# Forward weave dealt anew: row transposes of the attention sweep moved behind the row sums, and a 64-token projection tile, in a fused forward and backward kernel

## The chip, the cores and the metric

The kernel runs on one core of one Trainium2 chip. The metric is the device time of one execution in microseconds (us), the median of several runs. The engines are named as the profile names them: PE is TensorE (matmuls), PEld its weight loads, DVE is VectorE, ACT is ScalarE, POOL is GpSimd, SP is the queue that issues most DMAs. `L82` is line 82 of the kernel before.

## The reference

The reference returns the output of a gated mix of two attentions and the gradients of eleven inputs. `A` is multi-query attention with 32 heads of 18 channels over 2048 tokens; `B` is a recurrent attention with 32 heads of 128 channels over 64 segments of 32 tokens, in which eight memory rows go from one segment to the next:

```python
g = _sigmoid((x * gate_w).sum(-1, keepdims=True))
a = _A_ref(x, A_wq, A_wk, A_wv, A_wo)
b = _B_ref(x, B_mem0, B_Wq, B_Wk, B_Wv, B_Wo, B_seg_len)
return g * a + (1 - g) * b
```

The recurrence in `_B_ref`, where `mem` makes each segment wait for the one before:

```python
for s in range(n_seg):
    xs = x[:, s * seg_len:(s + 1) * seg_len, :].copy()
    h = jnp.concatenate([mem, xs], axis=1)
    q = jnp.einsum('btd,dhe->bhte', h, Wq)
    k = jnp.einsum('btd,dhe->bhte', h, Wk)
    v = jnp.einsum('btd,dhe->bhte', h, Wv)
    scores = jnp.einsum('bhqe,bhke->bhqk', q, k) * scale
    scores = jnp.where(mask[None, None], scores, -1000000000.0)
    p = _softmax(scores, axis=-1)
    o = jnp.einsum('bhqk,bhke->bhqe', p, v)
    o = jnp.einsum('bhte,hed->btd', o, Wo)
    mem = o[:, :M, :].copy()
    outs.append(o[:, M:, :])
```

The gradients come from `jax.vjp` of this function.

## The kernel before

The work stands in stages that follow each other. Inside the stages named here the order on each engine is the order in which the Python code emits it.

**Token projection** (`b_proj`, lines 229 to 259). Products of 128-token tiles with the weights of B: sixteen tiles of `dO`, then `XT0 = 5` tiles times k, v and q, fifteen items. An item has eight PSUM tiles `p_pb` of 128x512, each of four matmuls over full 128-row slices and one over a 64-row tail; four such tiles are computed, then copied by DVE and ACT in turn into `p_tok` (two buffers). SP writes `p_tok` to DRAM (`kx_dram`, `vx_dram`, `qx_dram`) at the start of the next item, the last one at line 258. The tokens from 640 on are not projected here.

**Forward weave** (`weave`, line 283). Two generators take turns: `b_chain_fwd`, the recurrence of B, with 64 segments of sixteen pieces, and `a_pass1`, the attention sweep of A, with 64 blocks of sixteen steps. Place p of a segment is piece p of the chain followed by one step of the sweep (step 16s+p+2). One sweep step n emits: scores of the next step (`a_S`, one buffer in PSUM), products `a_dP`, the exponential of the next step on ACT (`a_E`, L1881), two products on DVE (`a_W`, L1914), and twelve accumulating matmuls of step n-1 (`a_acc`). So the scores of a step wait until the exponential of the step before has read `a_S`.

The pieces of the chain that matter: place 0 forms the memory rows (`row_sums`), places 1 to 3 project k in halves `("k", 0)` in PSUM tile `c_pj` and `("k", 1)` in `c_x`, 4 to 6 project q, 6 and 7 transpose, 7 to 11 project v, 8 and 9 form the scores in `px` (a `c_x` tile), place 10 forms the softmax row sums `den` there with two matmuls against a block matrix, DVE takes the reciprocal `c_rd` (L521), POOL scales (`c_pn`, L523) and expands the probabilities to block form (`c_PBm`, then `c_PBx`, both L261); place 12 multiplies them with the values (`po`, `c_x`), PBx first. Places 13 to 15 project the output (`c_pj`). `c_x` and `c_pj` have one buffer each.

A projection unit `proj("k", j, kts)` emits four matmuls of 128x32 by 512 columns for each entry of `kts`.

The chain also carries, in the 24 rows of a segment that its 8 memory rows leave free, the projection of tokens that the first stage left out (`ride`, `put_ride`, the copies in `rows_copy`): 24 tokens a segment from token 640 on.

When a block of the sweep ends, ACT copies `a_acc` to `a_acs`, and `a_post` finishes the block during the next one, piece by piece: at step 3 of sixteen (place 1) it transposes the first half of `a_acs` (`half(0)`: two 128x128 float32 transposes into `c_x`, copied to `a_tk` by ACT); at step 10 (place 8) it loads the block's queries by two DMA transposes; at step 14 (place 12) it transposes the second half (into `c_pj`, copied by DVE); at step 15 (place 13) come the small products on POOL, which read `a_tk`, and the stores. For the last block all of that follows the sweep, on DVE, with its queries loaded into the memory of `a_W`.

**Bulk of B** (`b_bulk`, lines 691 to 964). Starts after the weave: for 128 groups of four heads in 128-token tiles it transposes q, k, dO and v, forms probabilities, outputs and gradients. At its start DVE zeroes four block tiles (`mB`, L675), SP issues the loads of the first four chunks (a chunk is four groups) in the order of lines 926 to 932, and the loop over groups starts. The step of group t transposes v of group t-2, multiplies the memory values `x_vmB` for group t-3 and the memory keys `x_kmB` for t-5.

After these stages come the backward weave, the gradients of the weights and the last products; the change doesn't touch them.

Of the kernel before, what the change touches and what calls it, by code (L numbers as in the profile page):

```python
# [16 lines left out]
P = 128  # L17
# [29 lines left out]
class Kern:  # L47
# [49 lines left out]

    XT0 = 5

# [130 lines left out]
    def b_proj(self, items, n0, n1, sp, psum, extra):  # L230
        nc = self.nc
        due = []
        for n in range(n0, n1):
            w, tt = items[n]
            for m in range(n, n + 3):
                self.proj_load(items, m, sp)
            extra(n)
            for args in due:
                nc.sync.dma_start(*args)
            xt = self.px.pop((w, tt))  # L240
            Wt = self.WoT if w == "dO" else self.W[w]
            tok = sp.tile([P, J], BF16, name="p_tok", bufs=2)
            for c2 in range(2):
                cs = (2 * c2, 2 * c2 + 1)
                pb = {(c, j): psum.tile([P, 512], F32, name="p_pb", bufs=8) for c in cs for j in range(2)}
                for c, j in pb:
                    for kt in range(4):
                        self.mm(pb[c, j][:], lhsT=xt[:, kt, :],
                                rhs=Wt[0][:, kt, (2 * c + j) * 512:(2 * c + j + 1) * 512],
                                start=(kt == 0), stop=False)  # L250
                for c, j in pb:
                    r = slice(64 * j, 64 * j + 64)
                    self.mm(pb[c, j][:], lhsT=xt[r, 4, :], rhs=Wt[1][r, c, :], start=False, stop=True, tp=(64 * j, 0))
                for c, j in pb:
                    self.evac(tok[:, (2 * c + j) * 512:(2 * c + j + 1) * 512], pb[c, j][:], use="vs"[j])
            due = [(self.xtok[w][tt * P:(tt + 1) * P, :], tok[:])]
        for args in due:
            nc.sync.dma_start(*args)
# [84 lines left out]
    def b_chain_fwd(self, keep, sp, psum):  # L343
        nc = self.nc
        NSEG = self.NSEG
        hm = self.hm
        hx = keep.tile([P, 3, 64], F32, name="c_hx")
        PBm = keep.tile([P, 8, 64], BF16, name="c_PBm")
# [6 lines left out]
        def ride(s):  # L355
            t0 = self.XT0 * P + 24 * s
            return t0, max(0, min(24, self.T - t0))
# [55 lines left out]
        for s in range(NSEG):  # L413
# [50 lines left out]
            if not last:  # L464
                put_ride(s + 1)
            proj("k", 0, (0, 1))
            yield
            proj("k", 0, (2, 3, 4))
            proj("k", 1, (0,))
            if wt is not None:  # L470
# [5 lines left out]
            yield  # L476
            proj("k", 1, (1, 2, 3, 4))
            yield
# [20 lines left out]
            proj("v", 0, (2, 3))  # L499
            px = psum.tile([P, 192], F32, name="c_x", bufs=1)  # L500
            ps, den = px[:, 0:P], px[:, P:192]
# [16 lines left out]
            self.mm(den, lhsT=self.blockones[:], rhs=Et[:, 0, :], start=True, stop=False)  # L518
            self.mm(den, lhsT=self.blockones[:], rhs=Et[:, 1, :], start=False, stop=True)
            rd = sp.tile([P, 64], F32, name="c_rd", bufs=1)  # L520
            nc.vector.reciprocal(rd[:], den)  # L521
# [147 lines left out]
    def b_bulk(self, wp, vp, kp, sp, psum):  # L669
# [3 lines left out]
        mB = {w: [wp.tile([P, 4, 4, E], BF16, name=f"x_{w}mB{i}") for i in range(2)] for w in ("k", "v")}  # L673
        for t in mB["v"] + mB["k"]:
            nc.vector.memset(t[:], 0.0)  # L675
        mT = {}
# [248 lines left out]
        later = {}  # L925
        load(0, ("q", "k", "mT", "dO"))
        load(1, deep)
        load(0, ("v", "vB", "kB"))
        load(1, ("v", "vB", "kB"))
        load(2, deep + ("mT", "v"))  # L930
        for c in range(3, BQ):
            load(c, deep)
        for t in range(NG + 6):
# [4 lines left out]
            for n, st in order:  # L938
# [5 lines left out]
                if st in after and t - n >= 0 and (t - n) % 4 == 3:  # L944
                    c = (t - n) // 4
                    for w, wait in after[st]:
                        later.setdefault(t + wait, []).append((c + (BQ if w in deep else 3 if w in ("mT", "v") else 2), (w,)))
                        if wait == 0:
                            load(*later[t].pop())
            if t % 4 == 2 and t // 4 - 2 in range(NTT // 4):  # L950
                self.dl_rows(t // 4 - 2, sp, psum)
# [912 lines left out]
    def a_pass1(self, keep, sp, psum, xps):  # L1864
# [78 lines left out]
    def a_post(self, b, acs, sp, psum, dl_all):  # L1943
# [6 lines left out]
        def queries():  # L1950
            qt = sp.tile([P, 2, 2, P], BF16, name="a_qt", tag="a_W" if end else "a_qt", bufs=2 if end else 1)
            src = self.qs_blk(b, 0)
# [4 lines left out]
        def half(hf):  # L1957
            pt = psum.tile([P, 2, P], F32, name=("c_x", "c_pj")[hf], bufs=1)
            for j in range(2):
                nc.tensor.transpose(pt[:, j, :], acs[:, (2 * hf + j) * P:(2 * hf + j + 1) * P], self.identF[:])  # L1960
            self.evac(tk[:, :, :, 32 * hf:32 * hf + 32], pt[:].rearrange("p t (g c) -> p t g c", c=32), use="sv"[hf])
# [37 lines left out]
        for w in range(2):  # L1999
            eng.tensor_copy(r4[:, :, :, w, :], rl[:, w].rearrange("p t (a i) -> p a t i", i=2))  # L2000
        q4 = qt[:].rearrange("p a t (b c) -> p (a t b) c", c=32)
        eng.tensor_tensor(out=q4, in0=q4, op=ALU.mult,
                                in1=r4[:].rearrange("p a t w i -> p (a t w i)").unsqueeze(2).to_broadcast([P, 16, 32]))
        dq_.dma_start(self.qs_blk(b, 1).rearrange("a p c -> p a c"), qt[:].rearrange("p a t x -> p a (t x)"))

# [360 lines left out]
```

## Time and profile before

| what | value |
|---|---|
| time, median of 3 runs | 5284.89 us (5282.66 to 5288.88) |
| time of the profiled execution | 5276.59 us |
| its span (first to last instruction) | 5274.6 us |

Busy time of the engines in stretches of the profiled execution, us, with the granted PE clock:

| stretch, us from the start | stage | length | PE | DVE | ACT | POOL | clock |
|---|---|---|---|---|---|---|---|
| 133.5 to 390.1 | token projection | 256.6 | 254.0 | 78.8 | 66.0 | 7.8 | 1.00 |
| 391.3 to 2029.6 | forward weave | 1638.3 | 1576.7 | 1419.8 | 1358.2 | 906.6 | 1.00 |
| 2030.9 to 2050.4 | weave to bulk | 19.5 | 4.1 | 11.1 | 1.3 | 11.7 | 0.55 |
| 2050.4 to 2600.0 | bulk of B, most of it | 549.6 | 518.5 | 412.5 | 356.6 | 399.6 | 0.99 |
| 2600.0 to 5274.6 | the rest | 2674.6 | 2539.1 | 1599.5 | 1452.1 | 1186.5 | 0.99 |

A row of the timeline has the start in us, the busy time in us, the engine, the line, the operation, output and inputs, their shapes, how many instructions were merged, and in brackets the idle time before it and what ended it. Matmul ends are modelled, so the distance between starts tells more than the busy time. All matmuls of the helper `mm` stand at L82, all bfloat16 transposes at L87; the tile names tell them apart.

### The profile page before, as it was taken

Reading aid. Unit: us, or ns where it says so; the run is one execution under the profiler, and the core shown is the slowest. Engines: PE = TensorE matmul, PEld = TensorE weight load, DVE = VectorE, ACT = ScalarE, POOL = GpSimd, SP = SyncE. Lnnn points to the kernel's source line nnn. Section 1 sums busy time; section 2 is a strip of 40 time slices with the busy share of each in tenths; the row PEclk is TensorE's granted clock in tenths of the full one; section 3 lists DMA queues with packets and bytes.
Section 4 is the critical chain, followed back from the end, with each engine's and each line's share of the span. In section 5 each row is a group of like instructions: output and inputs, shape, how many; then the busy total and the mean of one; then the engine's idle time right before and its main releaser. Section 6 shows DMA issues by size and latency. Waiting matters only on the chain.

```text
span 5274.6 us, 213519 instructions
## 1 busy us (share of the span) xinstructions
PE 4994.6 (95%) x90945; PEld 2898.4 (55%) x90945; DVE 3589.9 (68%) x7121; ACT 3295.0 (62%) x4757; POOL 2553.8 (48%) x4853
## 2 busy tenths in 40 slices
PE   7999999999999998999879999999999999999999
PEld 4335555555555555777635555555554467764444
DVE  5338888888888887777778888888888831111212
ACT  4228888888888886666668888888887732110100
POOL 2005555555555555777736666666654421222213
PEclk8999999999999999999989999999999999999999
DMA  6756556655665445888866989988977769966653
GB/s 225 236 198 133 145 140 141 148 141 138 141 145 131 118 108 181 254 246 251 262 178 177 200 200 196 200 198 198 202 166 143 149 160 233 282 222 213 198 187 106
DMA packets 1119994, 961.15 MB, mean 182 GB/s; under 512 B 689966, under 2 KB 947959, under 8 KB 1109438
## 3 DMA queue, kind: packets, MB, share of 16 engines
q1 hardware_dynamic: 1020318, 709.18, 54.8%
q0 software_dynamic: 98576, 238.16, 15.0%
q8 instruction: 712, 11.67, 1.0%
q14 instruction: 244, 2.00, 0.1%
q10 hardware_dynamic: 144, 0.15, 0.0%
HBM read 521.16 MB, written 357.96 MB: 167 GB/s over the span
## 4 chain that ended last, share of the span: by engine, by line
PE 71%; ACT 9%; issue 5%; DVE 4%; DMA 4%; POOL 3%; SPq 1%; POOLq 0%; ACTq 0%; DVEq 0%
PE w_acc L82 11%; PE r_pj L82 7%; PE b_S L82 6%; PE a_S L82 6%; ACT b_E L2054 5%; PE a_acc L82 5%; PE c_pj L82 5%; PE b_acc L82 5%; PE r_x L82 5%; PE p_pb L82 4%; PE c_x L82 4%; ACT a_E L1881 3%; PE y_pdx L82 2%; PE x_tr L87 2%; PE x_po L82 1%
## 5 line engine op out<-in xcount | busy, mean ns | idle before, releaser
L2077 DVE TENSOR_TENSOR b_dS<-b_dP,b_E 128x512 bf16<-128x512 f32 x2048 | 1315.1, 684 | 220.9 <-issue 87.1
L1914 DVE TENSOR_TENSOR a_W<-a_dP,a_E 128x512 bf16<-128x512 f32 x2048 | 1313.9, 684 | 205.6 <-issue 73.0
L2054 ACT ACTIVATE b_E<-b_S 128x1024 bf16<-128x1024 f32 x1024 | 1048.8, 1024 | 284.2 <-PE b_dP L82 197.9
L1881 ACT ACTIVATE a_E<-a_S 128x1024 bf16<-128x1024 f32 x1024 | 1049.9, 1025 | 237.4 <-PE a_dP L82 193.2
L82 PEld LDWEIGHTS <-b_QS 32*128 32x128 bf16 (+1 forms) x8192 | 271.1, 92 | 521.2 <-issue 466.6
L82 PE MATMUL r_pj<-WT,r_dT 128*32 128x288 bf16 x12288 | 495.7, 286 | 3.4 <-issue 3.4
L82 PE MATMUL b_S<-b_KV,b_QS 32*128 32x512 bf16 x2048 | 405.1, 382 | 92.8 <-ACT b_E L2054 62.0
L82 PE MATMUL w_acc<-w_d,w_h 128*128 128x512 bf16 (+1 forms) x2400 | 475.0, 379 | 0.0
L82 PE MATMUL a_S<-a_QD,l_KV 32*128 32x512 bf16 x2048 | 399.3, 381 | 41.6 <-ACT a_E L1881 19.8
L82 PE MATMUL b_acc<-b_dS,b_QS 128*32 128x512 bf16 x2048 | 422.8, 392 | 0.1
L82 PE MATMUL a_acc<-a_E,l_VK 128*32 128x256 bf16 x8192 | 412.1, 278 | 5.0
L82 PE MATMUL b_acc<-b_E,b_QS 128*32 128x512 bf16 x2048 | 405.7, 393 | 0.0
L82 PE MATMUL b_dP<-b_KV,b_QS 32*128 32x512 bf16 x2048 | 402.2, 388 | 0.0
L82 PE MATMUL a_dP<-a_QD,l_KV 32*128 32x512 bf16 x2048 | 398.3, 385 | 0.2 <-DVE a_W L1914 0.2
L82 PEld LDWEIGHTS <-r_dT 128*32 128x32 bf16 x12288 | 336.3, 97 | 92.9 <-issue 6.3
L82 PEld LDWEIGHTS <-w_h 128*128 128x128 bf16 (+1 forms) x2688 | 229.3, 100 | 258.9 <-issue 9.6
L82 PEld LDWEIGHTS <-l_KV 32*128 32x128 bf16 x4096 | 149.9, 91 | 287.4 <-issue 263.9
L82 PE MATMUL a_acc<-a_W,l_WK 128*32 128x256 bf16 x4096 | 291.4, 273 | 0.4 <-DVE a_W L1914 0.3
L79 ACT CAST w_o<-w_acc 128x512 bf16<-128x512 f32 x54 | 31.7, 586 | 384.6 <-PE w_acc L82 374.8
L82 PEld LDWEIGHTS <-l_VK 128*32 128x32 bf16 x8192 | 128.9, 94 | 236.9 <-issue 233.1
L77 DVE CAST w_o<-w_acc 128x512 bf16<-128x512 f32 x54 | 37.3, 692 | 313.5 <-PE w_acc L82 298.7
L1100 POOL TENSOR_TENSOR r_kb<-r_ks,bmask 128x512 bf16<-128x512 bf16 x176 | 188.7, 1072 | 105.2 <-DMA r_ks<-px_dram 49.5
(489 smaller groups left out, 10559.6 us busy)
## 6 DMA issues: line engine op xcount, KB each, us to landing
b_QS<-qs_dram SPq DMA_DIRECT2D x256, 256.0 KB
dOx_dram<-p_tok SPq DMA_DIRECT2D x16, 1024.0 KB
c_vx<-vx_dram SPq DMA_DIRECT2D x64, 256.0 KB
krow_dram<-c_k POOLq DMA_DIRECT2D x64, 256.0 KB, 2.9
qrow_dram<-c_q POOLq DMA_DIRECT2D x64, 256.0 KB, 4.4
vrow_dram<-c_v POOLq DMA_DIRECT2D x64, 256.0 KB, 6.3
x_q<-qx_dram SPq DMA_DIRECT2D x32, 512.0 KB
x_k<-kx_dram SPq DMA_DIRECT2D x32, 512.0 KB
```

Source lines behind the costliest of these rows:

```text
L77: nc.vector.tensor_copy(out, in_)
L79: nc.scalar.copy(out, in_)
L82: return self.nc.tensor.matmul(out, lhsT, rhs, start=start, stop=stop, tile_position=tp, skip_group_check=True)
L87: return self.nc.tensor.transpose(out, in_, self.identB[b:b + nrows, b:b + nrows], tile_position=tp)
L1100: nc.gpsimd.tensor_tensor(out=B[:], in0=a[:].unsqueeze(2).to_broadcast([P, 4, 4, SEG]), in1=self.bmask[:, :, 0].unsqueeze(1).unsqueeze(3). ...
L1881: nc.scalar.activation(E_[n][:], S.pop(n)[:], ACT.Exp, scale=SCALEA)
L1914: nc.vector.tensor_tensor(out=W_[n][:, i, :], in0=dP[i][:], in1=E_[n][:, i, :], op=ALU.mult)
L2054: nc.scalar.activation(E_[n][:], S.pop(n)[:], ACT.Exp, scale=SCALEA)
L2077: nc.vector.tensor_tensor(out=D_[n][:, i, :], in0=dP[i][:], in1=E_[n][:, i, :], op=ALU.mult)
```

## The change

It does five things.

1. The ride starts at token `X0 = 576`. The fifth projection tile then has 64 tokens: its items k, v and q write two 512-column halves to the two halves of the partitions of one PSUM tile (matmuls of 128x64 at `tile_position` (0, 64j), tails of 64x64), four `p_pb` tiles instead of eight, copied by DVE and ACT in turn, and stored by two DMAs with runs of 1 KB instead of one with runs of 8 KB. Rides go on to segment 61 instead of 58.
2. `half(0)` of the block's post-processing leaves place 1. The `c_x` tile of the chain's scores becomes 448 columns wide, and its last 256 columns take the two transposes at place 10, behind the row sums `den` and ahead of the reciprocal. Its query load stays at step 10.
3. The units of the projection of k are dealt anew: before 2, 4, 4 units at places 1, 2, 3, after it 3, 4, 3.
4. At place 10 POOL expands `c_PBx` ahead of `c_PBm`.
5. Between weave and bulk: the queries of the last block are loaded five steps before the end into a `c_wt` buffer (which the chain no longer uses then), its `a_tk` goes to a buffer of `a_E`; the bulk loads v of chunk 0 ahead of chunk 1 (`load`, called by `first(t)` at the end of the step of group t, issues the rest); the four memsets and the loads of `mB` are spread over the first four groups; and the first group's q and k transposes are copied by ACT.

```diff
-    XT0 = 5
+    XT0, X0 = 5, 576
...
+            T0 = P if w == "dO" else min(P, self.X0 - tt * P)
...
+                if T0 < 128:
+                    for c in cs:
+                        pb = psum.tile([P, 512], F32, name="p_pb", bufs=8)
+                        for kt in range(4):
+                            for j in range(2):
+                                self.mm(pb[64 * j:64 * j + 64, :], lhsT=xt[:, kt, 0:64],
+                                        rhs=Wt[0][:, kt, (2 * c + j) * 512:(2 * c + j + 1) * 512],
+                                        start=(kt == 0), stop=False, tp=(0, 64 * j))
+                        for j in range(2):
+                            r = slice(64 * j, 64 * j + 64)
+                            self.mm(pb[r, :], lhsT=xt[r, 4, 0:64], rhs=Wt[1][r, c, :], start=False, stop=True,
+                                    tp=(64 * j, 64 * j))
+                        self.evac(tok[:, c * 512:c * 512 + 512], pb[:], use="vs"[c % 2])
+                    continue
...
+            if T0 < 128:
+                due = [(self.xtok[w][tt * P:tt * P + 64, :].rearrange("t (c j e) -> t c j e", j=2, e=512)[:, :, j, :],
+                        tok[64 * j:64 * j + 64, 0:2048].rearrange("t (c e) -> t c e", e=512)) for j in range(2)]
+                continue
...
-            t0 = self.XT0 * P + 24 * s
+            t0 = self.X0 + 24 * s
...
-            proj("k", 0, (0, 1))
-            yield
-            proj("k", 0, (2, 3, 4))
-            proj("k", 1, (0,))
+            proj("k", 0, (0, 1, 2))
+            yield
+            proj("k", 0, (3, 4))
+            proj("k", 1, (0, 1))
...
-            proj("k", 1, (1, 2, 3, 4))
+            proj("k", 1, (2, 3, 4))
...
-            px = psum.tile([P, 192], F32, name="c_x", bufs=1)
+            px = psum.tile([P, 448], F32, name="c_x", bufs=1)
+            self.px_rest = px[:, 192:448].rearrange("p (t c) -> p t c", t=2)
...
             self.mm(den, lhsT=self.blockones[:], rhs=Et[:, 1, :], start=False, stop=True)
+            if s:
+                self.row_T()
             rd = sp.tile([P, 64], F32, name="c_rd", bufs=1)
             nc.vector.reciprocal(rd[:], den)
...
+            self.expand(PBx[:], pn[:, 0].rearrange("p (u q) -> p u q", q=8), 8)
             self.expand(PBm[:, :, 0:32].rearrange("p u (c q) -> p u c q", q=8), pn[:, 1].rearrange("p (u q) -> p u q", q=8), 8)
-            self.expand(PBx[:], pn[:, 0].rearrange("p (u q) -> p u q", q=8), 8)
...
-        for t in mB["v"] + mB["k"]:
-            nc.vector.memset(t[:], 0.0)
...
-            self.evac(o[:], pt[:], use="s" if w in ("dO", "v") else "v")
+            self.evac(o[:], pt[:], use="s" if w in ("dO", "v") or t == 0 else "v")
...
-        load(0, ("q", "k", "mT", "dO"))
+        load(0, ("q", "k", "mT", "dO", "v"))
         load(1, deep)
-        load(0, ("v", "vB", "kB"))
-        load(1, ("v", "vB", "kB"))
-        load(2, deep + ("mT", "v"))
-        for c in range(3, BQ):
-            load(c, deep)
+
+        def first(t):
+            if t < 4:
+                nc.vector.memset(mB["vk"[t // 2]][t % 2][:], 0.0)
+                load(t % 2, ("vk"[t // 2] + "B",))
+            if t == 0:
+                load(1, ("v",))
+            elif t == 1:
+                load(2, deep)
+            elif t == 2:
+                load(2, ("mT", "v"))
+                for c in range(3, BQ):
+                    load(c, deep)
...
-                if post is not None and kt in (3, 14):
+                if post is not None and kt == 14:
                     next(post)
+                if n == NP_ - 5:
+                    self.qt_last = self.cfs.tile([P, D], BF16, name="c_wt", bufs=2)[:, 0:512].rearrange(
+                        "p (a t x) -> p a t x", a=2, t=2)
+                    for a, src in enumerate(self.qs_blk(NB - 1, 0)):
+                        nc.sync.dma_start_transpose(self.qt_last[:, a], src)
...
         def half(hf):
-            pt = psum.tile([P, 2, P], F32, name=("c_x", "c_pj")[hf], bufs=1)
+            if hf or end:
+                pt = psum.tile([P, 2, P], F32, name=("c_x", "c_pj")[hf], bufs=1)[:]
+            else:
+                pt = self.px_rest
...
         if end:
-            qt = queries()
-        tk = sp.tile([P, 2, 4, 64], F32, name="a_tk", bufs=1)
-        half(0)
-        yield
+            qt = self.qt_last
+        tk = sp.tile([P, 2, 4, 64], F32, name="a_tk", tag="a_E" if end else "a_tk", bufs=3 if end else 1)
         if not end:
             qt = queries()
+            self.row_T = lambda: half(0)
+        else:
+            half(0)
         yield
         half(1)
```

More of the change, by code (lines that the diff above doesn't have):

```diff
@@ L240, in b_proj @@
             xt = self.px.pop((w, tt))
+            T0 = P if w == "dO" else min(P, self.X0 - tt * P)
+            assert T0 in (64, P)
             Wt = self.WoT if w == "dO" else self.W[w]
@@ L346, in b_chain_fwd @@
         hm = self.hm
+        self.cfs = sp
         hx = keep.tile([P, 3, 64], F32, name="c_hx")
@@ L949, in b_bulk @@
                             load(*later[t].pop())
+            first(t)
             if t % 4 == 2 and t // 4 - 2 in range(NTT // 4):
@@ L1950, in queries @@
         def queries():
-            qt = sp.tile([P, 2, 2, P], BF16, name="a_qt", tag="a_W" if end else "a_qt", bufs=2 if end else 1)
+            qt = sp.tile([P, 2, 2, P], BF16, name="a_qt", bufs=1)
             src = self.qs_blk(b, 0)
@@ L1957, in half @@
         def half(hf):
-            pt = psum.tile([P, 2, P], F32, name=("c_x", "c_pj")[hf], bufs=1)
+            if hf or end:
+                pt = psum.tile([P, 2, P], F32, name=("c_x", "c_pj")[hf], bufs=1)[:]
+            else:
+                pt = self.px_rest
             for j in range(2):
                 nc.tensor.transpose(pt[:, j, :], acs[:, (2 * hf + j) * P:(2 * hf + j + 1) * P], self.identF[:])
-            self.evac(tk[:, :, :, 32 * hf:32 * hf + 32], pt[:].rearrange("p t (g c) -> p t g c", c=32), use="sv"[hf])
+            self.evac(tk[:, :, :, 32 * hf:32 * hf + 32], pt.rearrange("p t (g c) -> p t g c", c=32), use="sv"[hf])
         if end:
-            qt = queries()
-        tk = sp.tile([P, 2, 4, 64], F32, name="a_tk", bufs=1)
-        half(0)
-        yield
+            qt = self.qt_last
+        tk = sp.tile([P, 2, 4, 64], F32, name="a_tk", tag="a_E" if end else "a_tk", bufs=3 if end else 1)
         if not end:
             qt = queries()
+            self.row_T = lambda: half(0)
+        else:
+            half(0)
         yield
@@ L2000, in a_post @@
             eng.tensor_copy(r4[:, :, :, w, :], rl[:, w].rearrange("p t (a i) -> p a t i", i=2))
-        q4 = qt[:].rearrange("p a t (b c) -> p (a t b) c", c=32)
+        qt = qt if end else qt[:]
+        q4 = qt.rearrange("p a t (b c) -> p (a t b) c", c=32)
         eng.tensor_tensor(out=q4, in0=q4, op=ALU.mult,
                                 in1=r4[:].rearrange("p a t w i -> p (a t w i)").unsqueeze(2).to_broadcast([P, 16, 32]))
-        dq_.dma_start(self.qs_blk(b, 1).rearrange("a p c -> p a c"), qt[:].rearrange("p a t x -> p a (t x)"))
+        dq_.dma_start(self.qs_blk(b, 1).rearrange("a p c -> p a c"), qt.rearrange("p a t x -> p a (t x)"))
     def sweep_first(self):
```

## The prediction

> **What bounds the kernel now.** The page comes first: PE is busy nearly all of the span, DVE and ACT two thirds of it. So time goes where PE has more work than a step allows, or waits.
>
> ```profile
> PE 4994.6 (95%) x90945; PEld 2898.4 (55%) x90945; DVE 3589.9 (68%) x7121; ACT 3295.0 (62%) x4757; POOL 2553.8 (48%) x4853
> ```
>
> Token projection, from PE's timeline near its end, and for comparison 128x64 matmuls from the last stage:
>
> ```profile
> 365.60 3.63 PE L82 MATMUL p_pb<-Wk,p_x 128*128 128x512 bf16 x16
> 369.16 0.60 PE L82 MATMUL p_pb<-Wkt,p_x 64*128 64x512 bf16 x4
> 369.70 3.63 PE L82 MATMUL p_pb<-Wk,p_x 128*128 128x512 bf16 x16
> ...
> 5265.15 0.38 PE L82 MATMUL f_big<-w_d,w_h 128*64 128x512 bf16 x1
> 5265.15 0.38 PE L82 MATMUL f_big<-w_d 128*64 128x512 bf16 x1
> 5265.37 0.38 PE L82 MATMUL f_big<-w_d,w_h 128*64 128x512 bf16 x1
> ```
>
> Half an item takes 369.70 - 365.60 = 4.10 us without a gap, an item 8.20: PE alone sets the pace (16 starts 0.216 apart; 0.10 more where the tiling changes to 64 rows and back). Two 128x64 matmuls on different halves of the columns start together, and the next pair 0.22 later: they run side by side.
>
> Forward weave, a segment in the timelines of PE, DVE and ACT. One start of `a_S` to the next is one place:
>
> ```profile
> 1002.26 0.39 PE L82 MATMUL a_S<-a_QD,l_KV 32*128 32x512 bf16 x2
> ...
> 1003.33 0.35 PE L82 MATMUL c_x<-c_PBx,c_vx 128*128 128x32 bf16 x8 [0.23 <-POOL c_PBx L261]
> ...
> 1004.11 0.39 PE L82 MATMUL a_S<-a_QD,l_KV 32*128 32x512 bf16 x2
> ...
> 1011.00 0.62 PE L82 MATMUL c_pj<-Wk,hm 128*32 128x512 bf16 x8
> 1011.55 0.44 PE L1960 MATMUL c_x<-identF,a_acs 128*128 128x128 f32 x2
> 1011.92 0.39 PE L82 MATMUL a_S<-a_QD,l_KV 32*128 32x512 bf16 x2
> ...
> 1025.42 0.23 PE L82 MATMUL c_x<-c_E,blockones 128*128 128x64 bf16 x2
> 1025.59 0.61 PE L82 MATMUL c_pj<-Wv,hm 128*32 128x512 bf16 x8
> 1026.23 0.39 PE L82 MATMUL a_S<-a_QD,l_KV 32*128 32x512 bf16 x2
> ```
> ```profile
> 1025.13 1.04 ACT L1881 ACTIVATE a_E<-a_S 128x1024 bf16<-128x1024 f32 x1
> ```
> ```profile
> 1026.38 0.55 DVE L521 RECIPROCAL c_rd<-c_x 128x64 f32<-128x64 f32 x1
> ```
>
> The distances between starts of the exponential, over segments 2 to 61, have a floor that nearly half of the places keep: 1.551 us, made of `a_S` to exponential 0.47, the exponential 1.02 and 0.06 to the next `a_S`. Above it (medians) stand place 1 with 1.598, places 2 to 5 with 1.631, place 10 with 1.570 and place 12 with 1.845; a segment takes 25.51. Place 12 is late since PE waits for the expanded probabilities (first two rows: 1.85 from `a_S` to `a_S`).
>
> Weave to bulk, from the timelines of SP, DVE and PE:
>
> ```profile
> 2035.93 0.50 SPq L709 DMA_DIRECT2D x_v<-vx_dram  x1
> ...
> 2042.46 8.21 SPq L700 DMA_DIRECT2D x_kmB<-km_dram  x4
> ```
> ```profile
> 2038.45 0.91 DVE L675 MEMSET x_vmB<- 128x1024 uint32 x1 [0.16 <-issue]
> ```
> ```profile
> 2050.39 0.61 PE L87 MATMUL x_tr<-identB,x_v 128*128 128x128 bf16 x4 [4.37 <-DMA x_v<-vx_dram]
> ```
>
> From 2030.9 to 2050.4 PE works 4.1 us. Two things end last: the four memsets, behind which the first q copies stand until 2042.5, then v, the ninth load, in flight from 2035.9 to 2050.4.
>
> **Projection tile (part 1).** An item becomes four tiles of four pairs and a tail pair. One tile: 4 x 0.216, a tail pair 0.226 (half of the measured 0.54 less two changes of tiling, 0.10 each, which I keep): 0.86 + 0.23 + 0.20 = 1.29; item 5.15. Three items: 3 x (8.20 - 5.15) = 9.1 us gained. Without changes of tiling an item is 4 x 5 x 0.216 = 4.3, gain 11.6; if pairs ran one after the other, 40 x 0.216 + 0.8 = 9.4, a loss of 3.7. I take 9.1, as the `f_big` rows are the same shape. Copies: two each of 0.68 (DVE) and 0.59 (ACT) lie under the matmuls. Stores: q3's 1 MB leaves at k4's start + 1.3 and takes about 5.7 (the k store that PE waited for at 285.4), so v4's copies start about 2 us late; eight PSUM tiles, of which an item now takes four, let PE run on. Uncovered that would cost 2. After the last matmul one copy of 0.59 ends it instead of two (1.29); one more issue on SP (0.33) stands ahead of the chain's first load (`c_rt`): 0.4 gained. Three more segments ride; segments without ride take 25.44 instead of 25.51: 0.2 lost. Their POOL copies and DMAs are in those 0.07. Sum **-9.3**.
>
> **Weave (parts 2 to 4), per segment.** Place 1 loses two transposes (0.37, start to start) and gains four matmuls (0.21): PE's work falls under the floor, -0.047. Place 2 keeps 16 matmuls. Place 3 has 12 instead of 16, as place 11, which stands at the floor: -0.08. Place 10: PE goes from `a_S` to `den` in 0.77, `den` 0.17, transposes 0.37, eight matmuls 0.43, change to `a_S` 0.11: 1.85, +0.28. It can't hide under the exponential, which ends at 1026.17, when PE would be 0.33 short of done; bounds +0.20 (the changes of tiling overlap) and +0.43 (nothing does). The ACT copy (0.37) runs from 1026.17, after the exponential, while PE is on the eight matmuls; the next exponential would start at 1026.98, so nothing is late.
>
> The reciprocal, though, waits for that copy in the built program's order (it waited for PE before). Copy end 1026.54, so it starts at 1026.60 instead of 1026.38: +0.22. Queued behind it on DVE is `a_W` of the step, ready at 1028.4, wanted by `a_acc` at 1028.6: covered by 0.2. POOL's chain follows (0.12 + 0.50 + 0.60 each): PBx, now first, at 1028.40 instead of 1028.8, PBm at 1029.0. PE comes to PBx at 1028.72, to PBm 0.2 later and waits 0.1: place 12 falls from 1.845 to about 1.58, -0.27 (bounds: -0.29, the floor; -0.20).
>
> The Trainium skill ("PSUM — Partial Sum Buffer", section on bank collisions) says that two engines may not use one bank and quadrant at once, even both reading, and that software has to keep them apart. By it the shared bank itself costs the 0.22 us, and a bank apart would spare the segment the 0.1 us of PBm; no row before shows it.
>
> Sum per segment -0.047 - 0.08 + 0.28 - 0.27 = -0.12; bounds -0.22 and +0.10. Times 62 segments: **-7.2**, bounds -13.6 and +6.
>
> **Weave to bulk (part 5).** The last block's query loads leave SP (2028.4 to 2030.9, held by `a_W`). In the built order the bulk's first loads then wait only for the chain's last uses of the memory they take: q and k of chunk 0 for place 2 or so of the last segment, dO for place 11 (about 2023). So v lands, counting the 14.4 us that it was in flight, by about 2039 at the latest, not 2050.4. DVE: its `a_tk` copy waited for POOL until 2033.4, now from about 2031.0; but `a_t` waits for POOL's last read of that buffer (2033.9), so the products end about 2036.7 instead of 2038.3. One memset (0.91 + 0.16) follows, not four; group 1's q copy comes at 2037.8 instead of 2043.5. Without the wait for v, PE's v transposes followed that copy by 2.3; one memset is now in between: 2041.1 against 2050.4, 9.3 gained. The other two memsets are not covered, as DVE works through the first groups: 2 x 1.05 lost. The first `x_P` may wait for POOL's stores (end 2043.1), which the memset hides. The `vmB` loads follow their memset (2037.7), four issues of 0.5 and some 3 us to land: 2043, wanted at 2044; uncovered 1 to 2. The two ACT copies of 0.59 run on an idle ACT. Sum **-7.2**; bounds -11 (all hidden) and -3 (v still ends it, one step earlier in its queue).
>
> **Sum.** -9.3 - 7.2 - 7.2 = -23.7 on a span of 5274.6; the profiled run (5276.6) would read 5253. It lies 8.3 under the median, so for a median I take 5284.9 - 23.7 = **5261.2**. Stages after it are only shifted.
>
> **Rivals.**
> (a) *Place 10 gives back what 1, 3 and 12 gain.* For it: 0.37 us of PE work is moved, not removed, and place 10 is over the floor already; PE's wait at 12 is 0.23, less than the 0.37. Against: places 1 and 3 fall below the floor. Weave 0 to +6; total -16.5 + 3: 5271.
> (b) *The handover moves to another wait* (`vmB` or the q copies behind the DVE products): part 5 yields 0 to 2; total about -17.5: 5267.
> (c) *Column pairs don't overlap in PSUM tiles that are filled by halves*: +3.7 for part 1; total -10.7: 5274. Against: the `f_big` rows.
> (d) *The other side: the reciprocal behind the copy.* ACT has a `c_v` copy (0.58), `c_E` (0.30) and the exponential in a row around place 10. If the copy, and with it the reciprocal, comes 0.5 later than now, `a_W` is ready at 1028.7, `a_acc` waits 0.1 or more at place 11, PBm comes 0.3 later and place 12 keeps its 1.85, while place 10 pays its 0.43: -0.13 + 0.43 + 0.1 = +0.40 a segment, +25; total +8.5: 5293. It decides for slower from +0.27 a segment on (16.5 / 62). For it: the wait is new and stands in the recurrence. Against: ACT is idle between 1026.17 and 1026.70.
> (e) *More than forecast*: bounds -11.6, -13.6, -11 at once: 5250.
>
> **How the numbers follow.** Forecast 0.60 (5253 to 5270), (a) 0.15, (b) 0.08, (c) 0.04, (d) 0.07, (e) 0.06. The range takes the forecast, (a), (b), (c) and part of (e): 5248 to 5277. A difference under 0.2% (10.6 us) can't be told from none. Faster: forecast, (b), (e) and two thirds of (a), 0.84; same: the rest of (a), (c) and a little of (d), 0.10; slower 0.06.
>
> **What would show it.** Items of about 5.1 us at the end of the projection and a first exponential near 381.7 instead of 391.3. In the weave place 1 and 3 at 1.55, place 10 at 1.85, place 12 at 1.58, a segment at 25.39. The first v transposes some 9 us after the last `a_acc` instead of 21. Wrong: a segment over 25.5, the reciprocal more than 0.4 after its old place, pairs of `p_pb` 0.43 apart, or an `x_tr` that still waits for a DMA.

## The result and the profile after

| what | before | after |
|---|---|---|
| median of 17 runs each, us | 5290.3 (5275.0 to 5312.2) | 5276.2 (5257.9 to 5288.6) |
| ratio after to before | | 0.9966 (95% interval 0.9955 to 0.9978) |
| profiled execution, us (span) | 5276.6 (5274.6) | 5281.9 (5280.2) |

The changed kernel is faster by 0.34%: on 5290.3 that is 18 us, by the interval 12 to 24 (the two medians lie 14.1 apart). Its profiled execution is nevertheless 5.6 us longer than that of before. So the first thing to do is to cut both spans at the same events and to ask which stretch moved. The cuts are starts of instructions in the two traces: the `k` item of the fifth token tile; the third exponential of the sweep; the nineteenth (one segment on); the one that opens the last segment; the last `a_acc`; the v transposes of the fourth group of the bulk; the first `b_S` of the backward weave; the end.

| stretch, us | before | after | difference |
|---|---|---|---|
| all ahead of the `k` item | 365.6 | 360.7 | -4.9 |
| last items of the projection, two steps of the sweep | 28.7 | 19.6 | -9.1 |
| first segment | 27.7 | 32.5 | +4.8 |
| segments 1 to 62 | 1583.6 | 1569.9 | -13.7 |
| last segment to the last `a_acc` | 23.7 | 26.1 | +2.4 |
| to the v transposes of the fourth group | 32.1 | 30.5 | -1.6 |
| rest of the bulk | 556.6 | 565.2 | +8.6 |
| backward weave to the end | 2656.7 | 2675.6 | +18.9 |

The five stretches that the change touches lose 17.2 us together, close to the measured 18. The last two rows hide it. The backward weave and what follows are not changed, and the rest of the bulk runs the same steps in all kernels; in the thirteen profiles of this study the last row lies anywhere between 2657 and 2687, the one above it between 554 and 566. The first row is unchanged code too, and lies between 360.7 and 365.6.

The page's busy line says nothing of this; PE is as busy as before:

```profile
PE 4991.9 (95%) x90945; PEld 2895.7 (55%) x90945; DVE 3589.3 (68%) x7113; ACT 3278.5 (62%) x4753; POOL 2561.0 (49%) x4871
```

**Projection.** The end of it in the timeline of PE, changed kernel:

```profile
375.22 1.05 PE L82 MATMUL p_pb<-Wq,p_x 128*64 128x512 bf16 x8
376.20 0.40 PE L82 MATMUL p_pb<-Wqt,p_x 64*64 64x512 bf16 x2
376.54 0.39 PE L82 MATMUL a_S<-a_QD,l_KV 32*128 32x512 bf16 x2
```

Eight matmuls take 0.98 from start to start of the next kind and the pair of tails 0.34: a tile takes 1.32 and an item 5.27 instead of 8.20. Column pairs run side by side. `a_S` follows without a wait; before it waited 0.61 for a copy.

**Weave.** A place 10 and its place 12 in the changed kernel, in the timelines of PE, then DVE, then POOL (compare the segment shown of before):

```profile
1010.98 0.39 PE L82 MATMUL a_S<-a_QD,l_KV 32*128 32x512 bf16 x2 [0.26 <-ACT a_E L1913]
...
1011.75 0.23 PE L82 MATMUL c_x<-c_E,blockones 128*128 128x64 bf16 x2
1011.82 0.42 PE L2000 MATMUL c_x<-identF,a_acs 128*128 128x128 f32 x2
1012.17 0.62 PE L82 MATMUL c_pj<-Wv,hm 128*32 128x512 bf16 x8
1012.72 0.39 PE L82 MATMUL a_S<-a_QD,l_KV 32*128 32x512 bf16 x2
...
1015.04 0.36 PE L82 MATMUL c_x<-c_PBx,c_vx 128*128 128x32 bf16 x8
1015.28 0.39 PE L82 MATMUL c_x<-c_PBm,c_v 128*128 128x64 bf16 x8
```
```profile
1012.80 0.56 DVE L545 RECIPROCAL c_rd<-c_x 128x64 f32<-128x64 f32 x1
```
```profile
1014.02 0.63 POOL L281 TENSOR_TENSOR c_PBx<-c_pn,bmask 128x256 bf16<-128x256 bf16 x1
1014.60 0.63 POOL L281 TENSOR_TENSOR c_PBm<-c_pn,bmask 128x256 bf16<-128x256 bf16 x1
```

From `a_S` to `a_S` place 10 takes 1.74. The transposes start 0.07 behind `den`, where before the eight matmuls of v started 0.17 behind it. Neither product of place 12 has a wait in brackets. Medians over segments 2 to 61, between exponentials: places 1 and 3 at 1.550, place 10 at 1.733, place 12 at 1.591, the segment 25.28 (before 25.51).

**Weave to bulk.** The long waits of PE from the last steps of the sweep to the fourth group, timeline of PE:

```profile
2003.92 0.27 PE L82 MATMUL a_acc<-a_E,l_VK 128*32 128x256 bf16 x1 [1.89 <-issue]
...
2016.84 0.59 PE L87 MATMUL x_tr<-identB,x_q 128*128 128x128 bf16 x4 [3.30 <-DVE x_qT L77]
...
2019.09 0.63 PE L87 MATMUL x_tr<-identB,x_v 128*128 128x128 bf16 x4
...
2024.48 0.29 PE L87 MATMUL x_S<-identB,x_P 128*128 128x128 bf16 x1 [3.88 <-POOL x_P L847]
...
2035.01 0.64 PE L82 MATMUL x_po<-x_v,x_PTB 64*64 64x128 bf16 x8 [3.41 <-POOL x_PTB L772]
...
2039.32 0.38 PE L87 MATMUL x_tr<-identB,x_v 128*128 128x128 bf16 x4
```

The last row is the fourth group's. Before, it was this one (timeline of PE of the kernel before; the first group's was 2050.39):

```profile
2061.37 0.39 PE L87 MATMUL x_tr<-identB,x_v 128*128 128x128 bf16 x4
```

The first v transposes come 10.3 us after the last `a_acc` (2008.85) and wait for no DMA; before it was 21.1. But three groups later 9.2 of these 10.9 us are gone: these three groups took 11.0 us before and take 20.2 now. POOL's timeline shows what it did instead of `x_P`:

```profile
2021.00 0.64 POOL L596 DMA_DIRECT2D memT_dram<-memT_hist  x1
2021.56 0.79 POOL L2032 DMA_DIRECT2D otok_dram<-a_ot  x1
2022.30 0.76 POOL L2038 DMA_DIRECT2D dqtok_dram<-a_dq  x1
2023.03 0.75 POOL L2046 DMA_DIRECT2D qs_dram<-c_wt  x1
2023.77 0.65 POOL L847 TENSOR_TENSOR x_P<-x_E,x_r 128x256 bf16<-128x256 bf16 x1
...
2032.92 0.61 POOL L909 TENSOR_TENSOR x_Y<-x_P,x_dl 128x256 f32<-128x256 bf16 x1 [5.97 <-DVE x_E L836]
2033.61 0.72 POOL L911 TENSOR_TENSOR x_dS<-x_X,x_Y 128x256 bf16<-128x256 f32 x1
2034.29 0.67 POOL L772 TENSOR_TENSOR x_PTB<-x_PT,tmask 128x256 bf16<-128x256 bf16 x1
```

The input of `x_P` was ready at 2019.5, but POOL issued the last stores of the weave first. Then `x_Y` waited 6 us, and `x_PTB`, for which PE waits, stands behind it. The profile names a DVE instruction of 2032.5 as the releaser; but of DVE `x_Y` needs only `x_dl`, which ended at 2028.0. In the trace it also waits for the semaphore of the store `memT_dram`. The two share no tile, so the reason must be memory that the store reads and `x_Y` takes over. In the kernel with part 5 alone the profile names that store (timeline of POOL of `part5_alone`):

```profile
2051.74 0.69 POOL L886 TENSOR_TENSOR x_Y<-x_P,x_dl 128x256 f32<-128x256 bf16 x1 [5.65 <-DMA memT_dram<-memT_hist]
```

### The profile page after: what moved, and what is told of

Same layout as the page of the kernel before. It is cut to its first block, busy times and chain, and to the rows that moved or that the text cites. A ratio compares the mean times of both kernels' runs of the same rounds, so it can differ in the third digit from the quotient of the medians.

```text
span 5280.2 us, 213541 instructions
## 1 busy us (share of the span) xinstructions
PE 4991.9 (95%) x90945; PEld 2895.7 (55%) x90945; DVE 3589.3 (68%) x7113; ACT 3278.5 (62%) x4753; POOL 2561.0 (49%) x4871
```

## Experiments

The stretches of the table above, in one profile of each kernel. A ratio is to the kernel before on the same chip.

| kernel | ratio (95%) | projection | first segment | segments 1 to 62 | last segment | to the fourth group |
|---|---|---|---|---|---|---|
| before | | 28.7 | 27.7 | 1583.6 | 23.7 | 32.1 |
| after | 0.9966 (0.9955 to 0.9978) | 19.6 | 32.5 | 1569.9 | 26.1 | 30.5 |
| part1_alone | 0.9989 (0.9974 to 1.0003) | 19.4 | 29.0 | 1584.0 | 23.7 | 31.3 |
| part24_alone | 0.9988 (0.9974 to 1.0002) | 28.9 | 27.0 | 1571.4 | 23.2 | 32.3 |
| part5_alone | 1.0002 (0.9987 to 1.0016) | 28.7 | 28.1 | 1582.8 | 26.6 | 29.7 |
| rt_first | 0.9952 (0.9929 to 0.9974) | 19.4 | 26.3 | 1570.5 | 24.4 | 29.4 |
| late_stores | 0.9965 (0.9951 to 0.9980) | 19.4 | 30.0 | 1571.2 | 25.5 | 30.3 |
| late_stores_act | 0.9968 (0.9952 to 0.9984) | 19.4 | 27.9 | 1570.7 | 24.3 | 29.9 |
| pbm_first | one run, 5266.3 us | 19.4 | 26.3 | 1583.4 | 24.8 | 29.5 |
| after_reciprocal | one run, 5389.6 us | 19.4 | 28.0 | 1692.2 | 26.2 | 29.8 |
| combined | 0.9942 (0.9921 to 0.9962) | 19.4 | 26.5 | 1571.2 | 24.2 | 21.7 |
| combined_pool | 0.9961 (0.9946 to 0.9976) | 19.4 | 26.5 | 1571.4 | 24.7 | 26.2 |
| combined_hold | 0.9965 (0.9952 to 0.9979) | 19.4 | 26.5 | 1571.0 | 25.5 | 25.0 |

### The parts alone

Each is the kernel before with the lines of the diff that belong to that part, and nothing else.

> The kernel before with part 1 alone (64-token projection tile, rides from token 576). Theory: the three items shrink from 24.6 to 15.8 us, as in the changed kernel, but the first load of the chain (c_rt) stands behind the two split stores of q and lands some 8 us after its issue instead of 5, so the first segment (exponential 2 to 18) takes about 32.5 us instead of 27.7: net gain about 4 us. Rival: the long first segment of the changed kernel was a disturbance of that one execution: first segment near 27.7, gain 8.6. Segments after it stay at 25.51.

The three items end 9.3 us earlier, as in the changed kernel. The first segment is 1.3 us longer than before, not 4.8: the truth lies between theory and rival. The time is lower by 0.1%, and the interval includes no change.

> The kernel before with parts 2, 3 and 4 alone (row transposes at place 10, k dealt 3-4-3, c_PBx first). Theory: the segment is 25.28 us as in the changed kernel, place 10 at 1.73, place 12 at 1.59; 62 segments give -14 us, first segment near 27.7, weave to bulk unchanged (32.1 us from the last a_acc to the v transposes of the fourth group). Rival: half of the gain came from part 1 or from the fewer waits it leaves: segment 25.4, -7.

Segments 1 to 62 take 12.2 us less, the median segment 25.30: theory right, rival out. Nothing else in the kernel moves.

> The kernel before with part 5 alone (weave to bulk). Theory (the wait moved): from the last a_acc to the v transposes of the fourth group about 30.5 us instead of 32.1, since POOL's queue of stores and the landing of the memory-row store hold the first groups; a stall of some 2.6 us at the last steps of the sweep, when the bulk's loads start early; total between -2 and +1. Rival (my forecast): 7 us less, 25 from the last a_acc to the fourth group, no stall.

Theory right: 2.4 us are gained to the fourth group, 2.9 are lost at the end of the sweep, and the time doesn't change. The same waits as in the changed kernel stand in the timeline of PE of this kernel:

```profile
2023.82 0.35 PE L82 MATMUL a_acc<-a_E,l_VK 128*32 128x256 bf16 x1 [2.11 <-issue]
...
2036.84 0.58 PE L87 MATMUL x_tr<-identB,x_q 128*128 128x128 bf16 x4 [4.28 <-DVE x_qT L77]
...
2043.62 0.29 PE L87 MATMUL x_S<-identB,x_P 128*128 128x128 bf16 x1 [3.02 <-POOL x_P L824]
...
2053.90 0.64 PE L82 MATMUL x_po<-x_v,x_PTB 64*64 64x128 bf16 x8 [3.16 <-POOL x_PTB L749]
```

### The first segment

```diff
                             elif n == len(items) - 4:
                                 k.load_A_kv(a2k)
+                                k.first_ride(a2k)
...
-        load_stage(0)
         put_ride(0)
```

`first_ride` issues the load of `c_rt` for the first four segments.

> The changed kernel with the chain's first load (c_rt) issued four items before the end of the projection, ahead of the last stores. Theory: the first segment falls from 32.5 to 27.7 or below (about 25.5 if nothing else is late), time -4.8 to -7. Rival: the first segment waits for something else behind the stores (the weight or v load), and stays over 31.

The first segment takes 26.3 us, 6.2 less than in the changed kernel and 1.4 less than before. In time the difference is not shown: the interval of this kernel (0.9929 to 0.9974) overlaps that of the changed one (0.9955 to 0.9978). In the changed kernel POOL's copy, and PE behind it, waited for this load (timelines of SP, POOL and PE):

```profile
377.26 1.17 SPq L278 DMA_DIRECT2D qx_dram<-p_tok  x2
378.48 0.79 SPq L387 DMA_DIRECT2D c_rt<-xT_dram  x1
```
```profile
386.67 0.26 POOL L394 COPY hm<-c_rt 128x96 bf16<-128x96 bf16 x1 [38.48 <-DMA c_rt<-xT_dram]
```
```profile
386.98 1.47 PE L82 MATMUL c_pj<-Wk,hm 128*32 128x512 bf16 x12 [4.17 <-POOL hm L394]
```

From its issue to the copy 8.2 us passed here, 5.3 in `part1_alone` and 4.9 before. Over all kernels: 26.3 to 32.5 (mean 29.0 of six) where `c_rt` stands behind the split stores, 27.0 to 28.1 (three) behind the one store of before, 26.3 to 26.5 (four) where it is loaded early. The profiled execution of the changed kernel was the worst of the six. The first two ranges overlap, and in `pbm_first` the copy came 3.6 us after the issue behind the same split stores; so the 1.4 us between their means is not shown to be the price of the splitting. What the runs do show is that an early load takes the long cases away. Which transfer holds the load in a bad case stays open.

Not all of the +4.8 is the load. PE waited 4.17 us for the copy instead of 0.24, which is 3.9 of it. In addition the granted clock stood at 0.50 for 13.6 us of this segment (379.4 to 393.0), against 6.8 before (394.4 to 401.2).

### The waits at the start of the bulk

```diff
+            if last:
+                nc.sync.dma_start(self.memT_dram[:], hist[:])
...
-            else:
-                nc.gpsimd.dma_start(self.memT_dram[:], hist[:])
...
             if t == 0:
                 load(1, ("v",))
+                for a in self.late:
+                    nc.sync.dma_start(*a)
```

`self.late` holds the last store of `oh_dram` and the three stores of the last block of the sweep.

> The changed kernel with the last stores of the sweep's end and of the chain's last output moved off POOL's queue: four are issued by SP behind the first v load of chunk 1, the memory-row store (memT_dram) is issued by SP at place 0 of the last segment. Theory: in the changed kernel PE's second and third long waits at the start of the bulk (3.9 us for x_P, which stands on POOL behind seven DMA issues, and 3.4 us behind x_Y, which waits for the landing of memT_dram) come from these stores; without them the v transposes of the fourth group come 6 to 7 us after those of the second instead of 13.5, and from the last a_acc to the fourth group it takes 24 us instead of 30.5; time -6. Rival: DVE's end products and memsets hold the groups anyway: gain under 2.

```diff
-            self.evac(o[:], pt[:], use="s" if w in ("dO", "v") or t == 0 else "v")
+            self.evac(o[:], pt[:], use="s" if w in ("dO", "v") or t < 2 else "v")
```

> The same, and the q and k transposes of the second group are copied by ACT like those of the first. Theory: PE's first long wait there (3.3 us for the x_qT copy, which stands on DVE behind the last block's products and a memset) goes too: the first v transposes come 7 us after the last a_acc instead of 10.3, the fourth group 21 us after it, time -9 against the changed kernel. Rival: the DVE chain of group 0 (mask, sum, reciprocal) becomes the next wait and the fourth group stays at 24.

Both gained under 1 us to the fourth group where 6 and 9 were expected (with ACT's copies the first v transposes came 9.6 us after the last `a_acc`, not 7: PE then waited 4.8 for the third group's q copy on DVE). The named waits did go: in `late_stores` PE waits neither for `x_P` nor for `x_PTB`. A new one took their place, in the timelines of PE and SP of `late_stores`:

```profile
2039.34 0.59 PE L82 MATMUL x_po<-x_kmB,x_mT 128*128 128x512 bf16 x1 [7.90 <-DMA x_kmB<-km_dram]
```
```profile
2020.16 5.91 SPq L964 DMA_DIRECT2D otok_dram<-a_ot  x1
...
2031.82 2.28 SPq L728 DMA_DIRECT2D x_kmB<-km_dram  x4
```

I had moved the stores into SP's queue without asking what stands behind them there: the load of the first memory keys, which also came behind the loads of chunk 2. Counted from the last `a_acc` it was issued 8.0 us later than in the changed kernel (22.4 against 14.4), and PE could start 7.5 us after the issue. Neither the theory nor the rival had it.

```diff
             if t < 4:
-                nc.vector.memset(mB["vk"[t // 2]][t % 2][:], 0.0)
-                load(t % 2, ("vk"[t // 2] + "B",))
+                nc.vector.memset(mB["vk"[t % 2]][t // 2][:], 0.0)
+                load(t // 2, ("vk"[t % 2] + "B",))
             if t == 0:
                 load(1, ("v",))
             elif t == 1:
-                load(2, deep)
+                for a in self.late:
+                    nc.sync.dma_start(*a)
             elif t == 2:
-                load(2, ("mT", "v"))
+                load(2, deep)
...
```

> The changed kernel with everything that the runs point to: c_rt loaded early, memT_dram stored by SP in the last segment, second group's q and k copied by ACT, the block tiles zeroed and loaded in the order in which they are used (vmB0, kmB0, vmB1, kmB1), the loads of chunk 2 behind the first two of them, and the last four stores on SP behind the loads of vmB0 and kmB0. Theory: the 8 us that PE waited for x_kmB with the stores ahead of it go, as its load is issued before stores and chunk 2; from the last a_acc to the v transposes of the fourth group 22 to 24 us instead of 30.5; with the first segment at 29.3 the time is 12 to 14 us under the changed kernel, ratio to before 0.994. Rival: DMA traffic of chunks 0 and 1 still delays a block tile (vmB0 or kmB0), the wait moves once more, 28 or more, ratio as with c_rt alone, 0.995 to 0.996.

> The same, but with the last four stores left on POOL's queue. Theory: x_P of the first group still stands behind POOL's issues and PE waits some 4 us for it, while the wait behind memT_dram (3.4 us) is gone: 26 to 27 us from the last a_acc to the fourth group, 3 more than with the stores on SP. Rival: equal to it, as DVE's end products hold the first groups anyway.

Here the theory holds: 21.7 us to the fourth group (22 to 24 expected) and 26.2 with the stores left on POOL (26 to 27). 3.94 of the 4.5 us between them are the one wait that comes back, in the timeline of PE of `combined_pool`:

```profile
2021.80 0.29 PE L87 MATMUL x_S<-identB,x_P 128*128 128x128 bf16 x1 [3.94 <-POOL x_P L850]
```

`combined` beats both kernels: 5261.1 us against 5294.1, 0.9942 of before. Its five stretches lose 32.8 us against the profile of before, by the ratio it is 31. Its interval overlaps that of the changed kernel a little (0.9962 against 0.9955), so that it is the better of the two rests on the stretches. It changes several things at once; what one of them gives inside it was tested for the place of the four stores alone (`combined_pool`) and, further down, for that of the loads of chunk 1 (`combined_hold`).

### The weave

```diff
-            self.expand(PBx[:], ...)
             self.expand(PBm[:, :, 0:32]..., ...)
+            self.expand(PBx[:], ...)
```

> The changed kernel with POOL's order put back: c_PBm ahead of c_PBx. Theory: PE comes to the product with c_PBx 0.6 us before it is ready less the 0.37 that the transposes no longer give it: place 12 rises from 1.59 to 1.8 us, the segment from 25.28 to 25.5, about +13 us: the swap, not the moved transposes, is what shortens place 12. Rival: the earlier place 1 and 3 leave POOL enough lead and place 12 stays at 1.6.

Place 12 goes back to 1.795 us, the segment to 25.50, segments 1 to 62 to 1583.4: +13.5. PE waits again where it waited before (timeline of PE):

```profile
1013.98 0.35 PE L82 MATMUL c_x<-c_PBx,c_vx 128*128 128x32 bf16 x8 [0.18 <-POOL c_PBx L281]
1014.18 0.39 PE L82 MATMUL c_x<-c_PBm,c_v 128*128 128x64 bf16 x8
```

In the kernel before PE waits for `c_PBx` in all 64 segments (0.23 us each, median), in the changed one in none. So without the swap the moved transposes and the new deal of k would have given nothing: -0.05 and -0.08 at places 1 and 3, -0.05 at place 12, +0.16 at place 10. (The one run of this kernel, 5266.3, lies inside the spread of single runs and decides nothing.)

Not run was the swap alone. Estimated from rows of before, it would give most of the gain: POOL's two expansions start 0.6 us apart, so PE would no longer wait for `c_PBx`; it comes to `c_PBm` 0.20 later, which leaves 0.03 of its 0.23. That is 0.2 us a segment, of the 0.22 that all three parts give together. Whether moving the transposes and dealing k anew add anything stays open.

```diff
-            if s:
-                self.row_T()
             rd = sp.tile([P, 64], F32, name="c_rd", bufs=1)
             nc.vector.reciprocal(rd[:], den)
+            if s:
+                self.row_T()
```

> The changed kernel with the two row transposes of place 10 issued behind the reciprocal of the row sums, which reads the same bank, instead of ahead of it. Theory: PE then has to wait for the reciprocal, which DVE starts only behind its product of the step: place 10 rises from 1.73 to 2.5 us or more, the segment to over 26.0, +45 us or more; the reciprocal itself starts no earlier, since DVE is busy until then anyway (the wait for the copy costs it 0.1 at most). Rival: the reciprocal gains 0.2, place 12 falls to 1.55, and the segment stays within 0.1 of 25.28.

Place 10 has a median of 3.25 us and segments 1 to 62 take 1692 us, +122: the theory's direction, more than its bound. PE stands until DVE has read the row sums (timelines of PE and DVE):

```profile
1026.47 0.23 PE L82 MATMUL c_x<-c_E,blockones 128*128 128x64 bf16 x2
1028.03 0.44 PE L2000 MATMUL c_x<-identF,a_acs 128*128 128x128 f32 x2 [1.32 <-DVE c_rd L543]
```
```profile
1027.42 0.55 DVE L543 RECIPROCAL c_rd<-c_x 128x64 f32<-128x64 f32 x1
```

The reciprocal starts 0.95 us behind `den`, as before (0.95); in the changed kernel, where it waits for the copy, 1.05 (medians). So waiting for the copy costs it 0.10 us; up to 0.95 DVE is at the step's products anyway.

### The stall at the end of the sweep

```diff
-        load(1, deep)
...
             if t == 0:
-                load(1, ("v",))
+                load(1, deep + ("v",))
```

> The combined kernel with the loads of q, dO and k of chunk 1 held back until after the first group's step (behind the load of vmB0), so that 1.5 MB less are in flight during the last two steps of the sweep. Theory: the stall of 0.7 to 2.4 us near the sweep's end, for which the trace names no releaser and which every kernel with early loads shows, comes from the traffic of these loads: it shrinks under 0.7 (0.60 is the largest distance between matmuls in the kernels without early loads), the last stretch of the sweep takes 23.7 us instead of 24.2, and the kernel is 0.5 to 1 us faster or no slower. Rival: the loads of chunk 0 alone (or nothing of the DMA) cause it, the stall stays, and kmB0, now behind chunk 1, lands late: 24 us or more instead of 21.7 from the last a_acc to the fourth group.

The rival was right about the stall and the time, not about which load is late: the stall stays (1.59 us of idle time, the same bracket `<-issue`), and q and k of chunk 1, not `kmB0`, hold PE for 1.1 and 2.4 us ahead of the third group's v transposes: 25.0 us to the fourth group instead of 21.7.

## Why the prediction was right, and where it was wrong

Forecast were -23.7 us and a median of 5261.2 within 5248 to 5277; measured are -18 (12 to 24 less) and 5276.2. The sign holds and the projection tile is right. That the sum comes near is luck: the weave gave 13.7 us where 7.2 less 0.2 for the riding segments were forecast, while the first segment lacks 5.2 and the way from weave to bulk 8.0. That 5276.2 lies in the range is luck too: it is 0.8 under its end, and the range stood on a median before of 5284.9, where the 17 runs give 5290.3.

- **Projection tile (-9.3).** Right: -9.1 in the profile of the changed kernel, -9.3 in all others that have it. The item is 5.27 us (5.15 forecast). The 0.226 for a pair of tails doesn't follow from the working given for it: half of 0.54 less two changes of 0.10 is 0.17, less one it is 0.22. Measured is 0.34 for the pair and the change back. Rival (c) is out.
- **What stands behind the stores (0.4 gained, 2 if uncovered).** Wrong. I counted the issue of the second store (0.33) but not that the chain's first load can land late: +4.8 in the profiled run, 29.0 us on the mean of six against 27.7 before. The step that failed is "one more issue on SP (0.33) stands ahead of the chain's first load": only the issue was costed, and the time from the load's issue to the copy, 4.9 before, was taken as fixed; it was 3.6 to 8.2.
- **Weave (-7.2).** The mechanism is right place by place: 1 and 3 fall to the floor, 12 to 1.59 (1.58 forecast), and the swap is what makes it so. The size is off by a factor of nearly two: -12.2 in `part24_alone`, -13.7 in the changed kernel. The term that was mis-sized is place 10, +0.28 forecast, +0.16 measured. I added the transposes to a `den` of 0.17 us; but 0.10 of that stood between `den` and the matmuls of v, and with the transposes in between they start after 0.07. Rival (a) is out.
- **The reciprocal behind the copy (+0.22, covered).** Mis-sized, without effect: +0.10, as DVE wasn't free earlier. Rival (d) is out in the changed kernel; `after_reciprocal` shows that the opposite order in the bank costs 1.5 us a segment. The rule of the Trainium skill ("PSUM — Partial Sum Buffer", section on bank collisions), that two engines must be kept apart in a bank, agrees with both traces: the reciprocal starts 0.03 after the end of the copy (median), and in `after_reciprocal` the transposes start 0.06 after the end of the reciprocal. But by the first order it costs 0.10 and not 0.22, and `c_PBm` isn't waited for.
- **Weave to bulk (-7.2).** Wrong; rival (b) happened, mostly by other places than the two it named (PE did wait 3.3 us for a q copy, but ahead of the v transposes, which came early even so). The first half is right: v no longer ends it and its transposes come 10.9 us earlier (9.3 forecast). The step that failed is "the first `x_P` may wait for POOL's stores, which the memset hides": PE waited 3.9 us for it. Not seen at all were `x_Y`, which waits for the memory-row store (PE 3.4 us behind it), and the stall near the end of the sweep, which all but one of the kernels with early loads show. Net +0.8 in the profile (-1.6 and +2.4), and 1.0002 for part 5 alone. `combined` shows the 7 us and more to be there once POOL's queue, SP's queue and the block tiles are ordered for it: 10.4 less to the fourth group than before.

So what was expected of part 5 was given back by the next waits. The weave's surplus made up about half of what part 5 and the first segment lack together (6.7 of 13.2).

## What to carry to other kernels

When the last wait of a stage is removed, list what each other queue still has to do at that point, POOL's and SP's DMA issues above all, and which memory is still being read by a store: here two waits of 3 to 4 us stood behind the one that was removed, and a third remained ahead of it. A store or load that is moved to another queue pushes back what stands behind it there; the loads that are needed first go first. And when a profile of the changed kernel is longer than that of before, cut both at the same events before believing either.

## What the runs showed of the hardware

- The code after the bulk, the same in all thirteen profiles, took 2657 to 2687 us. The gain of this change, 18 us, is smaller than that spread of 30; most of the spread is in the backward weave (1647 to 1675).
- In nine of the ten kernels with part 5 PE stands still 4 to 5 us ahead of the last `a_acc`, with no releaser in the trace: between two matmuls of one accumulation 0.99 to 2.38 us pass. In the three kernels without part 5 it is at most 0.60 in the last steps. The stall stands ahead of the same matmul each time, the 41st `a_acc` from the end, and it ends 1.4 to 1.6 us behind the end of a 16 KB packet of the DMA kind `instruction` (712 such packets in the changed kernel, one for 255 of PE's 181890 matmuls and weight loads). In the four kernels without the stall the packet ahead of that matmul ended 2.4 to 3.7 us before it. With part 5 that packet starts 9.1 to 10.5 us behind the one before it, without part 5 5.4 to 6.1. In `after_reciprocal` it is as late (9.9), but PE is too. So the traces fit instructions that reach PE late when the first loads of the bulk are in flight. No run moved that packet, though: holding back 1.5 MB of the loads left it as late (9.9), and what delays it stays open.
- The granted clock fell to 0.50 where PE had waited. At the start of the bulk it stayed there for 23.9 us before (2032.8 to 2056.7), for 23.9 in the changed kernel (2004.1 to 2028.0, from 0.2 us behind the end of the stall on) and for 3.4 more later, and for 10.2 in all in `combined`. In the changed kernel four v transposes took 0.43 us from start to start of the next kind there and 0.22 at full clock (2019.09, 2039.32), and the way from the stall to the last `a_acc` took 4.9 us instead of 4.2. So the 2.4 us lost at the end of the sweep are the stall and the lower clock behind it.
- The same store (`otok_dram`, 36 KB in short runs) took SP 0.38 us to issue in the weave, 5.91 among the loads at the start of the bulk in `late_stores`, and 2.70 in `combined`. POOL issued it there in 0.79 (changed kernel).
